# Another order of the side jobs in a long convolution, and the second normalisation of an MLP block one step sooner

## The chip, the cores and the metric

The kernel runs on one core of a Trainium2 chip. The metric is the device time of one execution in microseconds (us), the median of several runs. The engines are TensorE (PE in the profile, its weight loads PEld), VectorE (DVE), ScalarE (ACT), GpSimd (POOL) and SyncE (SP), which here only issues transfers.

## The reference

One transformer-like block on a sequence of S = 2048 rows and D = 640 channels, in float32. `mod` gives six rows of 640 from a condition vector.

```python
mod = (_silu(c) @ w_mod).reshape(c.shape[0], 6, 1, -1)
sa, ca, ga, sb, cb, gb = (mod[:, 0], mod[:, 1], mod[:, 2], mod[:, 3], mod[:, 4], mod[:, 5])
h = _layernorm(x, axis=-1) * (1 + ca) + sa
x = x + ga * _A_ref(h, A_k, A_v, A_shift_k, A_ssm_k, A_ssm_D)
h = _layernorm(x, axis=-1) * (1 + cb) + sb
x = x + gb * _B_ref(h, B_w1, B_b1, B_w2, B_b2)
```

`_A_ref` is a convolution: K goes through a causal convolution with four taps, is multiplied with V, and the product (kv) goes through a causal convolution as long as the sequence, one filter per channel, by FFT of length 4096; kv times a row D is added, and the result is multiplied with the normalised input. `_B_ref` is an MLP with 1728 hidden units: a matmul with w1, plus b1, ReLU, squared, a matmul with w2, plus b2.

## The kernel before

**Two stages.** The convolution stage treats the channels in five blocks of 128 (b = 0 to 4). The FFT is written as small matmuls with constant matrices. The MLP stage treats the rows in eight blocks of 256 (n = 0 to 7), and in each the hidden units in 14 steps (f = 0 to 13).

**The convolution of one block.** `unit_a` (line 383, `A` below) is one of eight transform units of a block: the filter's four (i = 1) and the data's four (i = 0), 64 small matmuls each into two PSUM tiles `pa`, which ACT copies to SBUF. `front` (eight per block) makes the spectra of filter (`h`) and data (`x`, line 398), ACT copies `h`, DVE multiplies twice, POOL subtracts and adds. `back` (four per block, line 464) is the first inverse transform and needs the products of two fronts. `unit_t` transposes (line 530, copied by ACT) and `unit_y` is the last inverse transform (line 541). In block 0 the filter's spectra are made ahead by `early_h`. The transform units of block b + 1 run in the tail of block b. In short, `A2.0.0` is the first data unit of block 2.

**Side jobs.** Everything else is a side job, called with its block and part. `kv_k`, `kv_v` transpose K and V on PE; `kv_s` applies the taps on DVE, `kv_m` multiplies and stores kv to DRAM; `kv_v` also issues the next loads of K and V. `load_h` and `load_x` load filter and kv of a block, for its transform units; `skip` adds the row D to the filter. `q_big`, `q_ut` load rows of q for `stats1`, the first normalisation's statistics; `stats1_end` takes the square root (line 303) and the reciprocal. `part_load`, `part_scale`, `part_add`, `mod_row`, `mod_col` compute the rows of `mod`. `load_xp`, `prep_a` (line 499, four ACTIVATEs), `prep_m`, `prep_p`, `gate`, `finish_near`, `finish_add` normalise q, gate the convolution's result and add it to q. `load_item`, `w_high`, `w_low` load the MLP's weights and split them into a high and a low part.

**What sets the order.** A table written out by hand gives the place of each side job: `FS(b, j)` is step j of the fronts of block b (j = 0 to 9), `GS(b, s)` is step s of its tail (s = 0 to 17). `UNITS` gives, per block, the tail steps of the transform units (seven; the eighth goes with step 9 of the fronts), of the eight `unit_t` and of the eight `unit_y`. In a tail step, `unit_y` and `unit_t` come first, then the transform units, then the table's jobs; for steps in `AFTER` the jobs come ahead of the transform units (in a step of the fronts, behind the `back`). At the end `keep_order` ties every engine's instructions to the order in which the program gave them. So each engine, and SP's queue with it, goes through its list in order, and an instruction that waits holds up those behind it.

**Queues and buffers.** All large transfers go through SP. `sp_dma` makes each transfer wait until the fourth one before it has landed:

```python
queued.append(nc.cur_bb.bb.instructions[-1].name)
if len(queued) > OUT:
    info = mybir.DependencyInfo(mybir.DependencyClass.Sync, mybir.DependencyReason.DATA)
    tc.add_manual_dep(nc.cur_bb.bb.instructions[-1], queued[-1 - OUT], info, reason="place in time")
```

PSUM has four buffers with the tag X (`pa`, `h`, `x`, V transposes), two with Y (`back`, `unit_y`, some K transposes) and two with T. The parts of `mod` and the staged weights share four SBUF buffers (tag STG). kv goes through two buffers, the halves of which `kv_k` writes and the store of `kv_m` frees.

**The MLP.** Step i of its loop issues the second matmuls of step i - 3 (`mlp_back`, line 790), the split of step i - 1's hidden values (`mlp_split`, an ACT copy into `hring` and a DVE subtraction), the first matmuls of step i (line 720, 15 of them), and their ReLU on ACT (line 752) and square on POOL. Beside them the next block is prepared: `load_x1` at f = 3, `stats2` at f = 5, square root and reciprocal at f = 6, then two `prep_hat` (line 672), each the normalisation of 128 rows, and from f = 8 on one `prep_xt` per step: two transposes on PE (line 685, one from each normalised half), scale and shift on DVE, split on ACT and POOL. In block 0 the two `prep_hat` are at f = 5 and 6, in the blocks n = 1 to 6 at f = 7 and 8.

## Time and profile before

| | |
|---|---|
| median of 3 runs | 703.28 us (702.06 to 704.84) |
| the profiled execution | 705.5 us, its span 703.7 us |
| convolution, MLP | up to about 292 us, from there to the end |
| TensorE busy | 662.0 us, 94% of the span |
| DVE, ACT, POOL busy | 334.6, 329.6, 311.2 us |
| granted TensorE clock, mean | 0.992 |
| moved by DMA | 74.76 MB |

The span runs from the first to the last instruction of the profiled execution; its time contains the little that lies around it. A row of the timeline gives the start, the duration, the engine and line, the operation with what it writes and reads, and how often it was merged; the brackets give how long the engine was idle before it and what ended the wait. "issue" stands for an idle engine that waits for nothing the profile shows.

### The profile page before, as it was taken

How to read it: one execution, taken by the hardware profiler on the slowest of the kernel's cores; microseconds unless marked ns; L12 is line 12 of the kernel's file. 1: busy time of each engine (PE TensorE's matmuls, PEld its weight loads, DVE VectorE, ACT ScalarE, POOL GpSimd, SP SyncE). 2: the span in 40 equal slices, each digit the busy share in tenths (PEclk: the TensorE clock that was granted, in tenths of full speed). 3: DMA queues.
4: the chain of work that ended last, by engine and by line, in shares of the span. 5: the costliest groups of instructions: out<-in, count | busy, mean ns of one | idle time of the engine just before them, and what ended most of it. 6: DMA issues, size and time to landing. Idle time of an engine off the chain costs nothing.

```text
span 703.7 us, 21084 instructions
## 1 busy us (share of the span) xinstructions
PE 662.0 (94%) x9164; PEld 634.2 (90%) x9164; DVE 334.6 (48%) x601; ACT 329.6 (47%) x688; POOL 311.2 (44%) x390
## 2 busy tenths in 40 slices
...
DMA packets 110960, 74.76 MB, mean 106 GB/s; under 512 B 48658, under 2 KB 96146, under 8 KB 110868
## 3 DMA queue, kind: packets, MB, share of 16 engines
...
## 4 chain that ended last, share of the span: by engine, by line
PE 83%; ACT 6%; DVE 5%; issue 3%; DMA 2%; POOL 1%; SPq 0%; DVEq 0%; ACTq 0%; POOLq 0%
PE acc L790 27%; PE h L720 25%; PE pa L383 5%; PE x L398 5%; PE qp L464 5%; PE y L541 5%; PE h L398 3%; PE t L530 2%; PE h L711 1%; PE xtp L685 1%; PE kt L239 1%; DVE wx L151 1%; ACT a L146 1%; PE vt L276 1%; PE gr L928 1%
## 5 line engine op out<-in xcount | busy, mean ns | idle before, releaser
L151 POOL TENSOR_TENSOR mtmp<-mtmp 128x256 f32<-128x256 f32 x112 | 71.4, 638 | 244.4 <-ACT mtmp L752 236.5
L720 PE MATMUL h<-xt,w_S 128*128 128x256 f32 x1290 | 167.5, 281 | 1.1 <-DVE w_S L157 1.1
L720 PEld LDWEIGHTS h<-xt,w_S 128*128 128x128 f32 x1290 | 161.7, 190 | 1.3 <-DVE w_S L157 1.3
L790 PE MATMUL acc<-w_S,hring 128*128 128x320 f32 x960 | 156.6, 311 | 0.2 <-DVE hring L157 0.2
L157 DVE TENSOR_TENSOR hring<-mtmp,hring 128x256 fp32r<-128x256 f32 x112 | 66.4, 593 | 162.6 <-ACT hring L146 162.6
L790 PEld LDWEIGHTS acc<-w_S,hring 128*128 128x128 f32 x960 | 142.0, 188 | 0.7 <-DVE hring L157 0.7
L752 ACT ACTIVATE mtmp<-h,b1t 128x256 f32<-128x256 f32 x104 | 49.4, 475 | 180.1 <-PE h L720 177.0
L146 ACT ACTIVATE hring<-mtmp 128x256 fp32r<-128x256 f32 x112 | 46.6, 416 | 48.5 <-POOL mtmp L151 47.5
L383 PE MATMUL pa<-wx,p 64*64 64x64 f32 x2560 | 49.7, 228 | 10.9 <-issue 5.3
L383 PEld LDWEIGHTS pa<-wx,p 64*64 64x64 f32 x2560 | 44.1, 141 | 17.2 <-issue 11.3
L146 ACT ACTIVATE a<-pa 128x512 f32<-128x512 f32 x80 | 43.6, 611 | 22.9 <-PE pa L383 22.8
L151 DVE TENSOR_TENSOR wx<-x,wx 128x512 f32<-128x512 f32 x64 | 41.0, 684 | 19.4 <-PE x L398 8.9
L541 PE MATMUL y<-wx,wx 128*64 128x64 f32 x1280 | 45.4, 226 | 4.5 <-ACT wx L146 2.7
L541 PEld LDWEIGHTS y<-wx,wx 128*64 128x64 f32 x1280 | 40.7, 139 | 9.5 <-issue 4.2
L687 DVE TENSOR_SCALAR we<-xtp,cbs 128x256 f32<-128x256 f32 x35 | 19.0, 544 | 61.1 <-PE xtp L685 61.1
L398 PE MATMUL x<-a,gb 128*64 128x128 f32 x640 | 43.8, 281 | 3.0 <-DVE wx L151 1.8
L398 PEld LDWEIGHTS x<-a,gb 128*64 128x64 f32 x640 | 37.7, 141 | 4.4 <-PE h L398 2.4
L261 DVE SCALAR_TENSOR_TENSOR KV<-kt,tap,KV 128x511 f32<-128x511 f32 (+2 forms) x48 | 35.9, 747 | 8.1 <-ACT ktail L146 6.3
L154 POOL TENSOR_TENSOR wm<-wm,wm 128x640 f32<-128x640 f32 x20 | 32.9, 1647 | 10.3 <-ACT wm L341 10.0
L146 ACT ACTIVATE q<-qp 128x512 f32<-128x512 f32 (+1 forms) x40 | 21.3, 585 | 33.1 <-PE qp L464 33.1
L157 POOL TENSOR_TENSOR we<-wx 128x256 f32<-128x256 f32 x20 | 15.8, 789 | 47.0 <-DVE wx L151 46.1
L398 PE MATMUL h<-a,gb 128*64 128x128 f32 x512 | 34.4, 275 | 0.6 <-ACT wx L146 0.6
...
## 6 DMA issues: line engine op xcount, KB each, us to landing
...
KV<-in_A_k_dram SPq DMA_DIRECT2D x20, 256.0 KB, 4.6
KV<-in_A_v_dram SPq DMA_DIRECT2D x20, 256.0 KB, 4.5
p<-in_A_ssm_k_dram SPq DMA_DIRECT2D x20, 256.0 KB, 4.9
p<-kv_d SPq DMA_DIRECT2D x20, 256.0 KB, 4.8
xp<-in_A_q_dram SPq DMA_DIRECT2D x20, 256.0 KB, 4.5
...
```

The source lines that it names most:

```text
L146: act.activation(o, i, AF.Copy)
L151: eng.tensor_mul(o, a, b)
L154: eng.tensor_add(o, a, b)
L157: eng.tensor_sub(o, a, b)
L261: dve.scalar_tensor_tensor(o, tk[:, : 512 - t], tap[:, b, t : t + 1], o, op0=ALU.mult, op1=ALU.add)
L383: pe.matmul(t[e][64 * r : 64 * r + 64, g].rearrange("p m d -> p (m d)"), pt[b][l, i, 8 * q + g, :], cw[l, r], start=True, stop=True,)
L398: pe.matmul(t[64 * a : 64 * a + 64, s + r], gb[:, g, r, a], AX[b][i][:, 2 * g + a], start=True, stop=True,)
L464: pe.matmul(t[a][:, u], gi[l, 4 * j + u, r], w[r][l, u % 2], start=(r == 0), stop=(r == 1),)
L541: pe.matmul(y[64 * h : 64 * h + 64, 4 * (g % 2) + i].rearrange("p c l d -> p (c l d)"), tss[g][:, i, 64 * r : 64 * r + 64], ca[:, r, h], s ...
L720: pe.matmul(hps[n, f][:m], WI[1, f][:, a, b], XT[n][:, x, b], start=(b == 0 and i == 0), stop=(b == NB - 1 and i == 2),)
L752: act.activation(r[:m], h[:m], AF.Relu, bias=b1t[:m, f : f + 1])
L790: pe.matmul(acc[2 * s + i], h[:, a, s * P : (s + 1) * P], w[:, y, i * 320 : (i + 1) * 320], start=(f == 0 and ti == 0), stop=(f == NF - 1 ...
```

## The change

In blocks n = 1 to 6 of the MLP both `prep_hat` calls stand in step f = 7. In the convolution about 110 of the side jobs stand in other steps or in another order within a step, seven more steps are in `AFTER` (20 become 27, not all the same), and `UNITS` has other steps for some transform units, `unit_t` and `unit_y`. No job is added or left out. The parts of the diff that the prediction speaks of:

```diff
@@ -938,140 +938,149 @@
...
-    at(FS(0, 1), (kv_k, 1, 0, "T"), (kv_v, 1, 0), (p_tile, 2))
-    at(FS(0, 2), (early_h, 0, 6))
-    at(FS(0, 3), (kv_s, 1, 0))
-    at(FS(0, 4), (early_h, 0, 7))
-    at(FS(0, 5), (kv_m, 1, 0), (kv_k, 1, 1, "T"))
-    at(FS(0, 6), (skip, 1))
-    at(FS(0, 7), (kv_s, 1, 1))
-    at(FS(0, 8), (kv_v, 1, 1))
-    at(FS(0, 9), (q_big, "XP0", 0))
-    at(GS(0, 0), (kv_m, 1, 1), (kv_k, 1, 2, "Y"), (kv_v, 1, 2), (q_big, "XP1", 4))
-    at(GS(0, 1), (kv_s, 1, 2))
-    at(GS(0, 2), (stats1, 0))
+    at(FS(0, 1), (early_h, 0, 6), (kv_k, 1, 0, "T"), (kv_v, 1, 0))
+    at(FS(0, 2), (p_tile, 2))
+    at(FS(0, 3), (early_h, 0, 7), (kv_s, 1, 0), (kv_m, 1, 0))
+    at(FS(0, 5), (skip, 1), (kv_k, 1, 1, "T"), (q_big, "XP0", 0))
+    at(FS(0, 8), (kv_s, 1, 1))
+    at(GS(0, 0), (kv_v, 1, 1), (kv_m, 1, 1), (kv_k, 1, 2, "Y"), (kv_v, 1, 2))
+    at(GS(0, 1), (kv_s, 1, 2), (stats1, 0))
+    at(GS(0, 2), (q_big, "XP1", 4))
...
-    at(FS(1, 1), (kv_k, 2, 2, "T"), (q_big, "UP1", 12), (stats1, 7))
-    at(FS(1, 2), (part_scale, 2, 0))
-    at(FS(1, 3), (skip, 2), (kv_s, 2, 2), (kv_v, 2, 2), (kv_m, 2, 2), (kv_k, 2, 3, "T"), (part_add, 2, 1, pool))
-    at(FS(1, 4), (kv_s, 2, 3), (kv_v, 2, 3), (part_scale, 2, 2), (part_load, 2, 4))
-    at(FS(1, 5), (kv_m, 2, 3), (part_add, 2, 2, pool), (part_scale, 2, 3), (part_load, 1, 0))
-    at(FS(1, 6), (q_ut,))
-    at(FS(1, 7), (part_add, 2, 3, pool))
-    at(FS(1, 8), (load_xp, 0))
-    at(FS(1, 9), (load_x, 2), (stats1, 13), (part_scale, 2, 4))
-    at(GS(1, 0), (p_tile, 3), (kv_k, 3, 0, "Y"))
-    at(GS(1, 1), (kv_s, 3, 0), (part_load, 1, 1))
+    at(FS(1, 2), (q_big, "UP1", 12), (part_scale, 2, 0), (part_load, 2, 4))
+    at(FS(1, 3),
+        (skip, 2), (kv_s, 2, 2), (kv_v, 2, 2), (kv_m, 2, 2), (kv_k, 2, 3, "T"), (q_ut,), (stats1, 7),
+        (part_add, 2, 1, pool),
+    )
+    at(FS(1, 5), (kv_s, 2, 3), (kv_v, 2, 3), (kv_m, 2, 3), (load_xp, 0), (part_scale, 2, 3))
+    at(FS(1, 6), (part_scale, 2, 2))
+    at(FS(1, 8), (stats1, 13), (part_add, 2, 2, pool), (part_load, 1, 0))
+    at(FS(1, 9), (part_scale, 2, 4))
+    at(GS(1, 0), (kv_k, 3, 0, "Y"), (part_add, 2, 3, pool), (part_add, 2, 4, pool))
+    at(GS(1, 1), (load_x, 2), (kv_s, 3, 0), (part_load, 1, 1))
...
     at(GS(1, 15),
-        (kv_m, 3, 3), (stats1, 8), (stats1, 10), (mod_row, 1), (part_scale, 0, 0), (part_scale, 0, 1),
-        (part_scale, 0, 2), (part_load, 0, 3), (part_load, 0, 4),
+        (kv_v, 3, 3), (kv_m, 3, 3), (mod_row, 1), (part_scale, 0, 0), (part_scale, 0, 1), (part_scale, 0, 2),
     )
-    at(GS(1, 16), (load_x, 3), (stats1_end,), (part_add, 0, 1, pool), (part_add, 0, 2, pool))
-    at(FS(2, 0), (load_h, 3), (load_xp, 1))
-    at(FS(2, 2), (part_scale, 0, 3), (prep_a, 0, 1))
-    at(FS(2, 3), (part_add, 0, 3, pool), (part_scale, 0, 4))
-    at(FS(2, 4), (part_add, 0, 4, pool), (prep_a, 0, 0), (prep_a, 0, 3), (prep_m, 0, 1))
-    at(FS(2, 5), (prep_m, 0, 0))
-    at(FS(2, 6), (skip, 3), (part_load, 3, 0), (part_load, 3, 2), (prep_a, 0, 2), (prep_m, 0, 3))
+    at(GS(1, 16), (stats1, 8), (part_add, 0, 2, pool), (part_load, 0, 4))
+    at(GS(1, 17), (load_h, 3), (stats1, 10), (load_xp, 1))
+    at(FS(2, 0), (load_x, 3), (part_scale, 0, 3))
+    at(FS(2, 1), (stats1_end,), (part_add, 0, 1, pool), (part_add, 0, 3, pool), (prep_a, 0, 1))
+    at(FS(2, 2), (part_scale, 0, 4))
+    at(FS(2, 3), (part_add, 0, 4, pool))
+    at(FS(2, 4),
+        (part_load, 3, 1), (prep_a, 0, 0), (prep_a, 0, 2), (prep_a, 0, 3), (prep_m, 0, 0), (prep_m, 0, 1),
+    )
+    at(FS(2, 5), (part_load, 3, 0), (prep_m, 0, 3))
...
-    at(GS(2, 1), (kv_s, 4, 0), (part_scale, 3, 1), (gate, 0, 1))
+    at(GS(2, 1), (p_tile, 4), (kv_s, 4, 0), (part_scale, 3, 1), (part_load, 3, 3), (gate, 0, 1), (gate, 0, 3))
...
-    at(GS(2, 14), (kv_v, 4, 3), (prep_a, 1, 3))
-    at(GS(2, 15), (prep_m, 1, 3), (gate, 1, 0))
-    at(GS(2, 16), (mod_col, 3, cbs[:, 0], 0.0), (part_load, 4, 1), (prep_p, 1, 3), (gate, 1, 1))
-    at(GS(2, 17), (kv_m, 4, 3), (part_load, 4, 3))
+    at(GS(2, 14), (kv_m, 4, 3))
+    at(GS(2, 15),
+        (mod_col, 3, cbs[:, 0], 0.0), (prep_m, 1, 2), (prep_a, 1, 3), (prep_m, 1, 3), (prep_p, 1, 3),
+        (gate, 1, 0),
+    )
+    at(GS(2, 16), (part_load, 4, 3), (prep_p, 1, 2), (gate, 1, 1))
+    at(GS(2, 17), (part_load, 4, 1))
...
-    AFTER = {GS(0, 9), GS(0, 11), GS(0, 14), GS(1, 1), GS(1, 4), GS(1, 12), GS(1, 13), GS(1, 14), FS(2, 9), GS(2, 1), GS(2, 2), GS(2, 9), GS(2, 10), GS(2, 15), GS(2, 17), GS(3, 2), GS(3, 5), GS(3, 10), GS(3, 12), GS(3, 16)}
+    AFTER = {GS(0, 3), GS(0, 4), GS(0, 6), GS(0, 9), GS(0, 11), GS(0, 14), GS(0, 15), GS(1, 1), GS(1, 3), GS(1, 7), GS(1, 8), GS(1, 10), GS(1, 11), GS(1, 13), GS(1, 14), GS(1, 15), FS(2, 9), GS(2, 4), GS(2, 9), GS(2, 15), GS(2, 17), GS(3, 1), GS(3, 2), GS(3, 4), GS(3, 12), GS(3, 14), GS(3, 15)}
     UNITS = [
-        ([0, 2, 4, 11, 11, 16, 16], [1, 3, 3, 5, 5, 6, 7, 9], [3, 4, 4, 6, 6, 8, 9, 10]),
-        ([1, 1, 5, 7, 9, 10, 12], [1, 3, 4, 6, 8, 11, 14, 14], [4, 6, 7, 10, 13, 14, 16, 17]),
-        ([1, 3, 5, 7, 8, 11, 14], [1, 3, 5, 7, 9, 11, 12, 15], [4, 6, 8, 9, 12, 14, 16, 17]),
-        ([0, 3, 4, 6, 9, 11, 14], [1, 3, 4, 7, 9, 11, 13, 14], [4, 6, 8, 10, 13, 14, 16, 17]),
-        ([], [1, 1, 2, 2, 5, 5, 6, 7], [4, 4, 5, 6, 6, 8, 8, 10]),
+        ([0, 1, 4, 11, 13, 16, 16], [1, 3, 3, 5, 5, 6, 7, 9], [3, 4, 4, 6, 7, 8, 8, 11]),
+        ([2, 2, 5, 5, 10, 10, 12], [1, 4, 4, 7, 8, 11, 13, 14], [4, 7, 7, 11, 13, 13, 16, 17]),
+        ([1, 2, 5, 7, 8, 11, 14], [1, 2, 5, 7, 9, 11, 13, 15], [4, 7, 8, 9, 13, 14, 16, 17]),
+        ([0, 3, 4, 6, 9, 11, 14], [1, 2, 4, 7, 8, 11, 14, 14], [4, 6, 8, 10, 11, 14, 17, 17]),
+        ([], [1, 1, 2, 2, 5, 5, 6, 6], [4, 5, 5, 6, 6, 8, 9, 9]),
     ]
...
@@ -1233,8 +1242,11 @@
                 if n and f == 6:
                     stats2_root(n + 1)
                     stats2_end(n + 1)
-                if f - (5 if n == 0 else 7) in (0, 1):
-                    prep_hat(n + 1, f - (5 if n == 0 else 7))
+                if n == 0 and f in (5, 6):
+                    prep_hat(1, f - 5)
+                if n and f == 7:
+                    prep_hat(n + 1, 0)
+                    prep_hat(n + 1, 1)
                 if f >= 8 and f - 8 < NB:
                     (prep_xt if n else prep_xt2)(n + 1, f - 8)
             if f >= 11 and f < 13:
```

164 lines of the change are left out of this document (86 added, 78 removed).

## The prediction

> **What bounds the kernel now.** I read the page's busy shares and the chain of waits first, then stretches of time, then who TensorE waits for.
>
> ```profile
> PE 662.0 (94%) x9164; PEld 634.2 (90%) x9164; DVE 334.6 (48%) x601; ACT 329.6 (47%) x688; POOL 311.2 (44%) x390
> PE 83%; ACT 6%; DVE 5%; issue 3%; DMA 2%; POOL 1%; SPq 0%; DVEq 0%; ACTq 0%; POOLq 0%
> 90.00:150.00 60.00, 57.19 (x1314) 51.25 (x1310) 39.57 (x78) 41.49 (x75) 32.44 (x45) 1.00 0.85 241
> 150.00:205.00 55.00, 52.72 (x1256) 47.87 (x1252) 39.34 (x61) 44.51 (x95) 45.25 (x52) 1.00 0.76 194
> 205.00:265.00 60.00, 56.73 (x1374) 52.27 (x1372) 46.36 (x59) 43.99 (x93) 48.66 (x47) 1.00 0.53 137
> 395.00:460.00 65.00, 63.68 (x488) 63.45 (x487) 20.82 (x43) 20.36 (x46) 21.70 (x27) 1.00 0.12 41
> ```
>
> (Columns of a stretch: its length, then busy time of PE, PEld, DVE, ACT, POOL, the granted clock, DMA share, GB/s.) TensorE is the bound everywhere. In the MLP (from 292 us on) the other engines are idle two thirds of the time, and 1.3 of 65 us are left on TensorE. In the convolution ACT, DVE and POOL are busy 54 to 82% as well, so an order can matter there; TensorE idles 2.3 to 3.3 us in each of these stretches. Only its idle time can be won, and the waits name it:
>
> ```profile
> PE xtp L685 <- ACT mtmp L672: 7.9, 6, 1.3
> PE pa L383 <- issue: 5.3, 5, 2.3
> PE y L541 <- ACT wx L146: 2.7, 4, 1.3
> PE x L398 <- DVE wx L151: 1.8, 3, 1.0
> ```
>
> (us in total, times, longest.) The largest, six times 1.3 us, is the place that the change's last hunk edits.
>
> **The MLP edit.** It removes nothing and adds nothing: the second of two `prep_hat` ACTIVATEs (line 672) is issued in step 7 of a block instead of step 8. The timeline of block 1, from step 7 to step 10, and the same wait one block later:
>
> ```profile
> 367.02 0.91 ACT L672 ACTIVATE mtmp<-x,nm,rs 128x640 f32<-128x640 f32 x1
> 367.85 0.42 ACT L146 ACTIVATE hring<-mtmp 128x256 fp32r<-128x256 f32 x1
> 368.15 1.93 PE L720 MATMUL h<-xt,w_S 128*128 128x256 f32 x15
> 370.18 0.47 ACT L752 ACTIVATE mtmp<-h,b1t 128x256 f32<-128x256 f32 x1 [1.91 <-PE h L720]
> 370.55 0.91 ACT L672 ACTIVATE mtmp<-x,nm,rs 128x640 f32<-128x640 f32 x1
> 371.51 0.33 PE L685 MATMUL xtp<-ident,mtmp 128*128 128x128 f32 x1 [1.32 <-ACT mtmp L672]
> 373.45 1.96 PE L720 MATMUL h<-xt,w_S 128*128 128x256 f32 x15
> 377.22 1.96 PE L720 MATMUL h<-xt,w_S 128*128 128x256 f32 x15
> 422.60 0.33 PE L685 MATMUL xtp<-ident,mtmp 128*128 128x128 f32 x1 [1.32 <-ACT mtmp L672]
> ```
>
> The second normalisation starts at 370.55 because it stands behind the ReLU of step 8, which waits for that step's matmuls; the transpose that reads it waits until 371.51. Step 8 lasts 373.45 - 368.15 = 5.30 us. Step 9 has the same 15 + 2 + 12 matmuls and lasts 377.22 - 373.45 = 3.77. The wait therefore costs 5.30 - 3.77 = 1.53 us per block, a little more than its 1.32 of shown idle. It occurs for n = 1 to 6, the six times of the wait row: block 0 keeps its old steps and the last block prepares nothing. Term: 6 x 1.53 = **-9.2 us**; the lower bound is the shown idle, 7.9.
>
> What hides the moved 0.91 us: after it ACT still has the split copy of step 7 (367.85 becomes 368.8) and then the ReLU at 370.18, before which it was idle 1.91 us. It now idles 1.0. The split copy is read by matmuls three steps later, some 10 us away, so nobody waits for it. With the cover gone, the ReLU itself would be late by the 0.91 and the wait would stay. The second normalisation is then ready at 368.8, and its transposes are wanted at 370.2: late next is nothing within 1.3 us.
>
> **The table of side jobs.** Laid side by side, the two orders have the same instructions on every engine; nothing is added or removed, DMAs included. On TensorE fewer than 20 of 211 groups change place. So the sum of work is unchanged and I cost places, from first to last.
>
> *End of the first front.* The value transposes of (1,1) stood ahead of the transform unit at 55.9 and now stand two units behind it; `early_h` and `kv_m(1,0)` come earlier on PE and DVE.
>
> ```profile
> 54.94 0.66 PE L276 MATMUL vt<-ident,KV 128*128 128x128 f32 x4
> 55.90 1.26 PE L383 MATMUL pa<-wx,p 64*64 64x64 f32 x64 [0.30 <-POOL p L154]
> 57.08 2.06 PE L464 MATMUL qp<-wx,gi 64*128 64x128 f32 x32
> 56.48 0.72 POOL L154 TENSOR_TENSOR wx<-wx 128x256 f32<-128x256 f32 x1
> ```
>
> The inverse matmuls at 57.08 need POOL's last product, done at 57.20 for their second half; it cannot be ready much earlier. Without the transposes TensorE arrives earlier, waits for POOL all the same, and pays their 0.5 afterwards: +0.5; up to +0.9 if `kv_m(1,0)`, now ahead of front 4 on DVE, passes its delay to POOL. `skip(1)` one step sooner takes the 0.30 away, but into the same wait.
>
> *The stall at 75 to 77 us.* It hangs on a store, through ACT:
>
> ```profile
> 63.77 3.07 SPq L138 DMA_DIRECT2D q<-in_A_q_dram  x4
> 68.53 0.33 SPq L138 DMA_DIRECT2D kv_d<-KV  x1
> 73.22 0.69 ACT L241 ACTIVATE KV<-kt,tap 128x512 f32<-128x512 f32 x1 [2.69 <-DMA kv_d<-KV]
> 75.00 1.15 PE L541 MATMUL y<-wx,wx 128*64 128x64 f32 x32 [1.29 <-ACT wx L146]
> 77.00 1.64 PE L541 MATMUL y<-wx,wx 128*64 128x64 f32 x32 [0.85 <-ACT wx L146]
> KV<-in_A_v_dram SPq DMA_DIRECT2D x20, 256.0 KB, 4.5
> ```
>
> ACT's order there is unchanged, and so is SP's last part: four q loads, then the store of (1,2), which by the rule of four in flight waits for the first of them. What changes is what that first q load waits for: the value load that goes out after the displaced transposes. They end near 57.1 + 2.0 + 1.1 + 0.6 = 60.8 instead of 55.6, and a value load lands 4.5 us later (the last row, a median). That puts the q load at 65.3 at the latest and the store 0 to 1.5 us later. The delay above ends in this same stall, so the two overlap: together **+0.9** (0 to +1.5).
>
> *The square root.* `stats1_end` moves from ahead of the third block's first front to behind its second.
>
> ```profile
> 146.72 1.28 ACT L303 ACT_TABLE_LOAD   x1
> 148.02 0.31 ACT L303 ACTIVATE rs<-st,eps_t 128x16 f32<-128x16 f32 x1
> 149.36 1.09 PE L398 MATMUL h<-a,gb 128*64 128x128 f32 x16 [0.55 <-ACT wx L146]
> 150.78 1.09 PE L398 MATMUL x<-a,gb 128*64 128x128 f32 x16 [0.32 <-DVE wx L151]
> 157.80 3.18 ACT L499 ACTIVATE KV<-xp,nm,rs 128x128 f32<-128x128 f32 x8
> 168.07 2.06 PE L464 MATMUL qp<-wx,gi 64*128 64x128 f32 x32
> ```
>
> Before, 148.33 - 146.72 = 1.6 us of ACT delay the first two copies of the block, and TensorE waits 0.55 + 0.32 = 0.87; at the MLP's ratio of lost to shown time (1.53 to 1.32) that is 1.0. Moved, the 1.6 delays the copy of the third front, whose four PSUM buffers come round again only two fronts later; TensorE needs some 3.5 us for two fronts and doesn't wait. But in step 4 twelve ACTIVATEs of `prep_a` now stand together where eight took 3.18: 4.8 us, so the copy of front 5 comes 1.6 later, and DVE, POOL and the inverse matmuls up to 168.07 follow it. Part of that meets slack; I take half of the 1.0 as kept: **-0.5** (-1.0 to +1.6, the last if the 1.6 is paid whole and the 1.0 not won). The Trainium skill, ScalarE: Activation LUTs, What ACT_TABLE_LOAD costs, counts a drain of some 1.4 us with each table load. The trace differs: the square root follows its load after 1.30. By the page I estimate the third copy 1.4 us later still and the term at about +0.5; the sum would be -8.6.
>
> *Small ones.* At two places the operation that ACT did ahead of the awaited one now comes behind it: `part_scale(3,1)` and the last `prep_a(1,3)`.
>
> ```profile
> 175.44 0.66 PE L276 MATMUL vt<-ident,KV 128*128 128x128 f32 x4 [0.43 <-ACT a L146]
> 198.81 1.15 PE L541 MATMUL y<-wx,wx 128*64 128x64 f32 x32 [0.36 <-ACT wx L146]
> ```
>
> **-0.8** (0 to -0.8).
>
> *Units due sooner.* `A2.0.0` follows `A2.1.3` directly, while `load_x(2)` goes from front step 9 to tail step 1 and `part_load(2,4)` waits for a buffer that POOL frees.
>
> ```profile
> 117.08 4.88 SPq L138 DMA_DIRECT2D p<-kv_d  x4
> 122.82 1.16 PE L383 MATMUL pa<-wx,p 64*64 64x64 f32 x64
> p<-kv_d SPq DMA_DIRECT2D x20, 256.0 KB, 4.8
> ```
>
> The transfers ahead of `load_x(2)` in SP's order are the same set, so it goes out near 117 as before; its first quarter lands near 117.1 + 4.8 = 121.9 and is wanted at 123.9. Zero, with 2 us in hand. The other moves (gates, loads, `finish_add`) I followed on each queue and found covered: DVE, ACT and POOL each have nearly 10 us or more free in every stretch quoted. "issue" stalls (5.3 us at `pa`) fall on dense runs of small matmuls; pairs are split here and joined there: 0, +-1.5.
>
> Sum for the convolution: 0.9 - 0.5 - 0.8 = -0.4; with the MLP -9.2 - 0.4 = **-9.6 us**: the profiled span goes from 703.7 to 694.1, its execution from 705.5 to 695.9. That execution lies 0.3% above the median of 703.28, within what runs scatter (702.06 to 704.84); the difference applied to the median gives **693.7 us**.
>
> **Rivals.** (1) *The new order removes most of the convolution's waits.* Those of the rows above (2.7 and 1.8 in the list, 0.55, 0.43 and 0.30 singly) sum to 5.8 us; with all gone, 703.3 - 9.2 - 5.8 = 688.3. For it: they are short and made by order. Against: 2.1 of them, at 75 to 77 us, hang on an unchanged order. 0.15. (2) *Side jobs in front of awaited copies on ACT eat most of the gain.* Each such place costs about the 1.6 us of the twelve ACTIVATEs; with four to five uncovered ones, 6 to 8 us, it is 700 to 702. For it: ACT is busy 44.5 of 55 us at 150 to 205. Against: ACT's order shifts by one or two places only. 0.08. (3) *SP is held.* If `part_load(2,4)` or `part_load(1,0)` waits for POOL longer than I read, key loads, `load_xp(0)` and `load_x(2)` all shift, and TensorE pays each us beyond the 2 in hand at `A2.0.0`. It decides the sign from a hold of 9.6 + 2 = 11.6 us; with 16, the time is 703.3 - 9.6 + 14 = 707.7. For it: both wait on adds that stand behind fronts on POOL. Against: those adds need no later load, and POOL idles 27 of 60 us from 90 to 150. 0.05. (4) *The edit doesn't remove the wait*, because the input of the second normalisation is late too: 703. Against: the first reads the same tile and statistics at 367.02 with no wait shown. 0.02.
>
> **Numbers.** The forecast has 0.70. Its own range is 690 to 699: the bounds above, from -1.8 to +3.1 together, and 1.5 of issue stalls either way. For 8 in 10 I reach over much of (1) and stop short of (2): 688.5 to 699. About 0.5% (3.5 us) is what a measurement here can tell from no change. Faster by more: 0.70 + 0.15 + a fifth of (2) = 0.87; same: 0.08; slower: 0.05.
>
> **What would show it.** Right: the wait of `xtp` for line 672 vanishes from TensorE's waits; step 8 lasts 3.8 us; line 672 runs twice in a row before the split copy; DVE's wait for `xtp` shrinks in no other step. The waits at 149 to 151 go, those at 75 to 77 stay, the store of (1,2) goes out at 68.5 to 70. Wrong: MLP blocks still last 422.60 - 371.51 = 51.1 us; or the convolution's end moves by more than 4 us either way; or `pa` waits for the kv_d loads near 124.

## The result, and the profile after

The changed kernel takes 692.89 us (median of 4 runs, 692.28 to 696.13); the kernel before, run beside it, 704.06 us (702.06 to 705.56). The ratio is 0.9857, with a 95% interval of 0.9826 to 0.9889: faster by 1.4%, with 1 outside the interval, and 0.8 us below the forecast. The profiled execution took 693.38 us, its span 691.6.

From the page of the changed kernel its busy times and the chain of waits; then its stretches of time, columns as in the prediction; then TensorE's waits:

```profile
PE 657.0 (95%) x9164; PEld 630.8 (91%) x9164; DVE 335.9 (49%) x601; ACT 330.1 (48%) x688; POOL 311.4 (45%) x390
PE 81%; DVE 6%; ACT 5%; DMA 4%; issue 2%; POOL 1%; DVEq 0%; POOLq 0%; ACTq 0%; SPq 0%
```

```profile
90.00:150.00 60.00, 53.93 (x1266) 48.51 (x1264) 38.40 (x75) 37.30 (x68) 30.75 (x43) 1.00 0.83 232
150.00:205.00 55.00, 53.76 (x1274) 48.55 (x1272) 44.17 (x63) 45.36 (x97) 46.94 (x51) 1.00 0.86 226
395.00:460.00 65.00, 65.00 (x498) 65.00 (x497) 20.82 (x45) 20.94 (x47) 20.77 (x28) 1.00 0.11 41
```

```profile
PE pa L383 <- issue: 6.1, 6, 2.0
...
PE pa L383 <- DMA p<-kv_d: 3.1, 2, 2.3
...
PE h L398 <- ACT wx L146: 1.5, 1, 1.5
```

Before, the list of waits was led by `xtp` with 7.9 us; now it has no row for `xtp` at all, and TensorE is busy for all 65 us of an MLP stretch instead of 63.68. In the convolution the wait of `h` for ACT's copy has grown from 0.6 to 1.5 us and moved on by one front, and from 90 to 150 us TensorE is busy 3.3 us less than before (the same stretch of time holds partly other work). On the chain ACT gives up a per cent and DMA takes two more. The timeline of block 1 of the MLP, answering to the one shown of before:

```profile
363.81 0.47 ACT L752 ACTIVATE mtmp<-h,b1t 128x256 f32<-128x256 f32 x1 [1.97 <-PE h L720]
364.18 1.73 ACT L672 ACTIVATE mtmp<-x,nm,rs 128x640 f32<-128x640 f32 x2
365.31 1.93 PE L720 MATMUL h<-xt,w_S 128*128 128x256 f32 x15
367.08 0.38 PE L685 MATMUL xtp<-ident,mtmp 128*128 128x128 f32 x2
367.34 0.48 ACT L752 ACTIVATE mtmp<-h,b1t 128x256 f32<-128x256 f32 x1 [1.12 <-PE h L720]
369.06 1.96 PE L720 MATMUL h<-xt,w_S 128*128 128x256 f32 x15
```

Both normalisations run in one row of 1.73 us and are ready at 365.91, 1.17 us before the first transposes at 367.08. Step 8 lasts 369.06 - 365.31 = 3.75 us; it was 5.30. From one block's first `xtp` to the next one's it is now 49.54 us, before 51.09.

Where the MLP begins, first before, then after (name, count, shortest, median and longest in ns, first and last start). I take the start of the `gr` matmuls, which make the MLP's gate row, as the border; the 292 us of the prediction are where they end:

```profile
L928 PE MATMUL gr<-w_gate x20: 432/432/537, 285.0 to 291.4; 128*128 128x320 f32 x20
```

```profile
L928 PE MATMUL gr<-w_gate x20: 432/432/537, 282.2 to 288.5; 128*128 128x320 f32 x20
```

From there to the end of the span it is 703.7 - 285.0 = 418.7 us before and 691.6 - 282.2 = 409.4 after: **-9.3 us in the MLP, -2.8 us in the convolution** by this pair of profiles. The second number isn't what it seems. The granted clock differs between these two executions in the early convolution (the number after the five busy times), first before, then after:

```profile
36.00:62.00 26.00, 25.32 (x468) 23.12 (x472) 15.88 (x25) 10.08 (x22) 14.38 (x27) 0.93 0.79 227
62.00:90.00 28.00, 23.47 (x692) 21.47 (x684) 19.11 (x41) 15.65 (x30) 3.88 (x12) 0.94 0.86 247
```

```profile
36.00:62.00 26.00, 25.50 (x542) 23.56 (x543) 17.97 (x29) 11.85 (x24) 15.63 (x31) 1.00 0.85 237
62.00:90.00 28.00, 24.58 (x680) 22.38 (x680) 18.60 (x41) 17.45 (x33) 4.70 (x14) 1.00 0.92 252
```

One pair of profiles cannot tell the order's part from the clock's part. The first experiments take the two halves of the change apart and give more executions of each order.

### The profile page after: what moved, and what is told of

The parts are those of the page before. It is cut to its first block, busy times and chain, and to the rows that moved or that the text cites. A ratio compares the mean times of both kernels' runs of the same rounds, so it can differ in the third digit from the quotient of the medians.

```text
span 691.6 us, 21100 instructions
## 1 busy us (share of the span) xinstructions
PE 657.0 (95%) x9164; PEld 630.8 (91%) x9164; DVE 335.9 (49%) x601; ACT 330.1 (48%) x688; POOL 311.4 (45%) x390
## 3 DMA queue, kind: packets, MB, share of 16 engines
q8 instruction: 72, 1.18, 0.7%
## 4 chain that ended last, share of the span: by engine, by line
PE 81%; DVE 6%; ACT 5%; DMA 4%; issue 2%; POOL 1%; DVEq 0%; POOLq 0%; ACTq 0%; SPq 0%
PE acc L790 27%; PE h L720 26%; PE qp L464 5%; PE pa L383 4%; PE x L398 4%; PE y L541 4%; PE h L398 3%; DMA wm<-in_w_mod_dram 3%; PE t L530 2%; PE h L711 1%; PE xtp L685 1%; DVE KV L261 1%; ACT wx L146 1%; DVE kacc L261 1%; PE vt L276 1%
## 5 line engine op out<-in xcount | busy, mean ns | idle before, releaser
L541 PE MATMUL y<-wx,wx 128*64 128x64 f32 x1280 | 43.9, 224 | 2.9 <-ACT wx L146 1.6
L398 PE MATMUL x<-a,gb 128*64 128x128 f32 x640 | 41.6, 274 | 3.3 <-DVE wx L151 2.1
L398 PEld LDWEIGHTS x<-a,gb 128*64 128x64 f32 x640 | 35.9, 137 | 4.9 <-PE h L398 3.0
L790 PE MATMUL acc<-w_WX,hring 128*128 128x320 f32 x192 | 31.4, 312 | 0.0
```

Source lines behind the costliest of these rows:

```text
L398: pe.matmul(t[64 * a : 64 * a + 64, s + r], gb[:, g, r, a], AX[b][i][:, 2 * g + a], start=True, stop=True,)
L541: pe.matmul(y[64 * h : 64 * h + 64, 4 * (g % 2) + i].rearrange("p c l d -> p (c l d)"), tss[g][:, i, 64 * r : 64 * r + 64], ca[:, r, h], s ...
L790: pe.matmul(acc[2 * s + i], h[:, a, s * P : (s + 1) * P], w[:, y, i * 320 : (i + 1) * 320], start=(f == 0 and ti == 0), stop=(f == NF - 1 ...
```

## The experiments

**The MLP edit alone.** The kernel before with only the last hunk:

```diff
-                if f - (5 if n == 0 else 7) in (0, 1):
-                    prep_hat(n + 1, f - (5 if n == 0 else 7))
+                if n == 0 and f in (5, 6):
+                    prep_hat(1, f - 5)
+                if n and f == 7:
+                    prep_hat(n + 1, 0)
+                    prep_hat(n + 1, 1)
```

> The kernel before with the last hunk alone: both second-half and first-half normalisations of the MLP's blocks 1 to 6 in step 7, the table of side jobs as before. Theory A (the MLP edit does what the prediction says, independent of the convolution): -9.2 us, ratio 0.987 (0.9855 to 0.9885); the stretch from the first gr matmul to the end is 409.4 us instead of 418.7, and TensorE has no wait for xtp left. Rival B (the whole gain of the change is made in the MLP, and the convolution's 2.8 us in the two profiles are only the lower granted clock of the profile before): -11.2 us, ratio 0.984. Beside it this run is a second look at the unchanged convolution: by A the first gr matmul starts at 284 to 285 us whatever the clock, by B at 282 to 283 once the clock is full.

Measured: ratio 0.9889 (0.985 to 0.9928). The `gr` matmuls begin at 284.3 us and the span is 693.7, so the MLP takes 409.4 us, to 0.1 us what it takes in the changed kernel. Theory A holds; B's 0.984 is just outside the interval.

**The table alone.** The changed kernel with the old `prep_hat` lines put back (the same hunk reversed).

> The changed kernel with the old place of the second normalisation (step 8), so only the table of side jobs and the units are changed. The prediction's sum for this part: -0.4 us, ratio 0.9994. By the two traces (start of the MLP at 282.2 instead of 285.0): -2.8 us, ratio 0.996. Rival (those 2.8 us were the granted clock of 0.93 and 0.94 in the profile before, between 36 and 90 us): 0, ratio 1.000. The waits at TensorE for the load of wm ahead of the second front's copy (1.46 us at 149.6) are in its profile in any case.

Measured: ratio 0.9979 (0.9953 to 1.0005), on 704.14 us some -1.5 us (-3.3 to +0.4). The prediction's -0.4 and the -2.8 of the two profiles are both inside; 0 is as well. The profiled execution is the longest of 12 (708.03 us), and the same convolution that ended at 282.2 above ends later than before the change:

```profile
L928 PE MATMUL gr<-w_gate x20: 432/432/537, 287.5 to 293.9; 128*128 128x320 f32 x20
```

The MLP takes 706.3 - 287.5 = 418.8 us, as before the change. So the MLP repeats to 0.1 us, and the convolution alone scatters by over 5.

**Place or step?** The kernel before, with the second normalisation still in step 8 but ahead of that step's ReLU:

```diff
+            if 0 < n < NC - 1 and f == 8:
+                prep_hat(n + 1, 1)
             mlp_front_end(n, f)
...
-                if f - (5 if n == 0 else 7) in (0, 1):
-                    prep_hat(n + 1, f - (5 if n == 0 else 7))
+                if n == 0 and f in (5, 6):
+                    prep_hat(1, f - 5)
+                if n and f == 7:
+                    prep_hat(n + 1, 0)
```

> The kernel before with the second normalisation still in step 8, but issued ahead of that step's ReLU and not behind it. Theory A (the wait is made by the place behind the ReLU in ScalarE's order): the same -9.2 us as the step sooner, ratio 0.987, no xtp wait, because it starts at about 368.3 in block 1 and is ready at 369.2, a us before its transposes are wanted at 370.2. Rival (a whole step of lead is needed, because its input or its buffer isn't free before): the xtp wait stays at 0.5 to 1.3 us in each of six blocks, ratio 0.992 to 1.000.

Measured: ratio 0.9889 (0.985 to 0.9927), span 693.7 with `gr` from 284.3, so 409.4 us again. ScalarE's order in block 1:

```profile
367.15 0.42 ACT L146 ACTIVATE hring<-mtmp 128x256 fp32r<-128x256 f32 x1
367.48 0.91 ACT L672 ACTIVATE mtmp<-x,nm,rs 128x640 f32<-128x640 f32 x1
369.48 0.47 ACT L752 ACTIVATE mtmp<-h,b1t 128x256 f32<-128x256 f32 x1 [1.10 <-PE h L720]
```

The normalisation fills time in which ScalarE waited for the step's matmuls. Its place behind the ReLU made the wait, not the step it is written in.

**How much cover there is.** The changed kernel with the second normalisation of step 7 issued one to three times more:

```diff
                     prep_hat(n + 1, 0)
                     prep_hat(n + 1, 1)
+                    for _ in range((n + 1) // 2):
+                        prep_hat(n + 1, 1)
```

> The changed kernel with the second normalisation of step 7 issued again, with the same result, once more in blocks 1 and 2, twice more in blocks 3 and 4, three times more in blocks 5 and 6 (0.87 us of ScalarE each). It measures the cover that the moved 0.9 us was said to have. Theory A (free up to the 1.1 to 1.2 us that ScalarE is idle ahead of the next ReLU and that the transposes have in hand): blocks 1 and 2 as long as in the changed kernel, blocks 3 and 4 longer by 0.6 to 0.8, blocks 5 and 6 by 1.5 to 1.7, xtp waits of 0.6 and 1.4. Rival (the matmuls read the late split copy or the late square sooner than three steps on): blocks 1 and 2 longer already. Rival (the transposes alone set it, the ReLU's delay is seen by nobody): the same lengths as in theory A, and no wait of TensorE but that for xtp.

Measured, from the first `xtp` of one block to that of the next: 49.54 and 49.56 us in blocks 1 and 2 (one more), 50.27 and 50.28 in blocks 3 and 4 (two more), 51.25 in block 5 (three more): +0, +0.7 and +1.7. TensorE's waits from the MLP's begin on:

```profile
PE xtp L685 <- ACT mtmp L672: 4.0, 4, 1.5
PE h L720 <- DVE w_S L157: 1.1, 1, 1.1
PE acc L790 <- DVE hring L157: 0.2, 1, 0.2
```

The sizes are those of theory A; the last two rows are in the changed kernel's profile with the same numbers. The only wait that grows is that for `xtp`. In the trace the ReLU of step 8 begins 2.72 us after its matmuls in block 3 and 3.67 in block 5, against 2.03 in the changed kernel (367.34 - 365.31), so it is 0.7 and 1.6 us late, and TensorE has no wait for that. So the third reading in the expectation fits: the transposes set the limit. What a late ReLU would cost alone was not tested, since TensorE is held about as long by the transposes.

**The changed kernel once more.**

> The changed kernel once more, for its scatter and a second profile: 692 to 696 us, ratio 0.986; from the first gr matmul to the end 409.4 us as in its first profile (an MLP without waits repeats to 0.1 us), its convolution's end anywhere from 281 to 288 us. If the granted clock sets the scatter, the profile with the lower clock between 36 and 90 us has the later end; if the stalls without a shown cause set it, the one with more of them.

Measured: ratio 0.9853 (0.9801 to 0.9906); span 695.4, `gr` from 286.0, so 409.4 again. The table gives, from the timelines of seven profiles, the time between the starts of the same matmuls. The last two columns are the sum of TensorE's waits marked "issue" from 40 us to the end of the convolution (to 0.1 us), and the granted clock from 36 to 62 and from 62 to 90 us.

| profile | up to block 3's first K transposes | block 1's tail, to the first front of block 2 | head of block 2, to its last inverse matmuls | from there to `gr` | `gr` | issue | clock |
|---|---|---|---|---|---|---|---|
| old order: before | 116.59 | 28.51 | 22.97 | 116.96 | 285.03 | 6.4 | 0.93, 0.94 |
| old: the MLP edit alone | 115.68 | 28.10 | 22.71 | 117.85 | 284.34 | 5.4 | 0.93, 1.00 |
| old: ahead of the ReLU | 115.55 | 28.20 | 22.71 | 117.87 | 284.33 | 5.6 | 1.00, 0.94 |
| new order: after | 111.50 | 31.19 | 24.75 | 114.73 | 282.17 | 5.6 | 1.00, 1.00 |
| new: after, once more | 114.91 | 28.51 | 23.97 | 118.58 | 285.97 | 7.4 | 0.91, 1.00 |
| new: the table alone | 117.39 | 29.97 | 21.77 | 118.39 | 287.52 | 8.8 | 0.93, 0.99 |
| new: normalisation repeated | 116.83 | 26.97 | 23.97 | 116.00 | 283.77 | 6.2 | 1.00, 0.93 |

Among the four of the new order the clock of 36 to 62 us and the stalls go with the end alike, so both readings of the expectation stand; the two were not separated. Variants that follow below say that neither alone accounts for the end: two with the full clock there end at 285.9 us, with 7.6 and 7.7 us of stalls (the square root in the gap, the additions later), and one with 4.7 us of stalls ends at 286.7, with a clock of 0.93 (the data load sooner). The means of `gr` are 284.6 for the old order and 284.9 for the new one. No gain of the new table shows here: it gains a little in the first and the last stretch and loses 0.8 to 0.9 us each, on the mean, in block 1's tail and in the head of block 2. The next experiments look for why. Timelines of the changed kernel (its first profile) at the places that they touch:

```profile
54.49 2.19 PE L464 MATMUL qp<-wx,gi 64*128 64x128 f32 x32
54.89 0.72 POOL L154 TENSOR_TENSOR wx<-wx 128x256 f32<-128x256 f32 x1
66.10 0.74 SPq L138 DMA_DIRECT2D kv_d<-KV  x1
72.24 1.15 PE L541 MATMUL y<-wx,wx 128*64 128x64 f32 x32 [0.60 <-ACT wx L146]
120.43 1.17 PE L383 MATMUL pa<-wx,p 64*64 64x64 f32 x64 [0.82 <-DMA p<-kv_d]
131.57 1.61 ACT L341 ACTIVATE wm<-wm,sg 128x640 f32<-128x640 f32 x2 [2.80 <-DMA wm<-in_w_mod_dram]
148.19 0.83 ACT L341 ACTIVATE wm<-wm,sg 128x640 f32<-128x640 f32 x1 [2.98 <-DMA wm<-in_w_mod_dram]
149.52 1.28 ACT L303 ACT_TABLE_LOAD   x1
149.56 1.09 PE L398 MATMUL h<-a,gb 128*64 128x128 f32 x16 [1.46 <-ACT wx L146]
150.82 0.31 ACT L303 ACTIVATE rs<-st,eps_t 128x16 f32<-128x16 f32 x1
```

**A scaling ahead of an awaited copy.** At 148.19 ScalarE stood 2.98 us at the load of part (0,3), with the copy of block 2's second front behind it; TensorE lost 1.46 us.

```diff
-    at(FS(2, 0), (load_x, 3), (part_scale, 0, 3))
-    at(FS(2, 1), (stats1_end,), (part_add, 0, 1, pool), (part_add, 0, 3, pool), (prep_a, 0, 1))
+    at(FS(2, 0), (load_x, 3))
+    at(FS(2, 1), (part_scale, 0, 3), (stats1_end,), (part_add, 0, 1, pool), (part_add, 0, 3, pool), (prep_a, 0, 1))
```

> The changed kernel with one job moved: the scaling of part (0,3) of the modulation, whose load lands at 148.2, stands behind the copy of block 2's second front instead of ahead of it. Theory S (each us that ScalarE stands at that load ahead of an awaited copy is paid by TensorE, and what follows the copy has slack, as the prediction said of the square root): the waits of 1.46 and 0.32 at 149.6 and 151.0 vanish, -1.8 us against the changed kernel. Theory D (the slack behind is used up: the scaling, the table load, the square root and the first four normalisations then hold the copy of the third front, which ends at about 153.4 instead of 153.9): only -0.5 us, the fifth front starts at about 153.4 instead of 154.0 and waits for the copy.

Measured: ratio 0.9892 (0.9858 to 0.9925), no gain in time. The waits at 149.6 and 151.0 are gone and the part up to the first inverse matmuls lasts 7.09 us instead of 9.31. But the fifth front now waits, and the part behind it lasts 16.88 instead of 15.44:

```profile
156.81 1.09 PE L398 MATMUL h<-a,gb 128*64 128x128 f32 x16 [1.33 <-ACT wx L146]
```

Of 2.2 us won 1.4 are given back at once. The head of block 2 is 0.8 us shorter, near theory D's 0.5 and not S's 1.8. That the edit took the first two waits away is not shown: the three other profiles of the new order in the table have the same 7.09 us without it. In the second profile of the changed kernel the scaling starts at 145.01 without a wait, because its load has landed by then.

**Why the third front's copy is late.** In that profile and in the second one of the changed kernel the copy stands behind four normalisations of q that wait for DVE. From the second profile of the changed kernel:

```profile
148.74 0.72 POOL L157 TENSOR_TENSOR we<-wx 128x256 f32<-128x256 f32 x1
148.80 2.88 DVE L305 SCALAR_TENSOR_TENSOR nm<-st,rs 128x16 f32<-128x16 f32 x1
149.43 0.72 POOL L154 TENSOR_TENSOR we<-wx 128x256 f32<-128x256 f32 x1
150.12 3.14 POOL L154 TENSOR_TENSOR wm<-wm,wm 128x640 f32<-128x640 f32 x2
151.72 1.65 ACT L499 ACTIVATE KV<-xp,nm,rs 128x128 f32<-128x128 f32 x4 [3.23 <-DVE nm L305]
153.89 1.09 PE L398 MATMUL h<-a,gb 128*64 128x128 f32 x16 [1.33 <-ACT wx L146]
```

The DVE operation has 16 columns; it took 0.28 us in the first profile of the changed kernel (from 151.45), here 2.88. It ends at 151.68, and the first of POOL's two additions, which lasts 1.53 us by itself, at 150.12 + 1.53 = 151.65. The experiment is the previous one with these two additions behind the products of the third and fourth fronts:

```diff
-    at(FS(2, 1), (part_scale, 0, 3), (stats1_end,), (part_add, 0, 1, pool), (part_add, 0, 3, pool), (prep_a, 0, 1))
+    at(FS(2, 1), (part_scale, 0, 3), (stats1_end,), (prep_a, 0, 1))
...
-    at(FS(2, 3), (part_add, 0, 4, pool))
+    at(FS(2, 3), (part_add, 0, 1, pool), (part_add, 0, 3, pool), (part_add, 0, 4, pool))
```

> The kernel of e4 with two of POOL's additions (parts (0,1) and (0,3)) behind the products of block 2's third and fourth fronts instead of ahead of them. In the profiles of e4 and of the second run of the changed kernel the small DVE operation nm<-st,rs (0.28 us in one profile) takes 2.17 and 2.88 us and ends with POOL's first addition, to 0.01 us; ScalarE's normalisation waits for it, the copy of the third front stands behind that, and TensorE waits 1.33 us at the fifth front. Theory P (DVE is held while POOL runs without a gap): nm ends with POOL's last product of the second front instead, 1.5 us sooner, lasts under 1 us, and the wait at the fifth front falls from 1.33 to 0.2 or none. Rival Q (the operation waits for something else, the square root's result or its own queue): nm as long as before, wait 1.3.

```profile
150.85 0.72 POOL L154 TENSOR_TENSOR we<-wx 128x256 f32<-128x256 f32 x1
150.94 0.67 DVE L305 SCALAR_TENSOR_TENSOR nm<-st,rs 128x16 f32<-128x16 f32 x1
164.84 0.49 PE L464 MATMUL qp<-we,gi 64*128 64x128 f32 x4 [0.72 <-POOL we L157]
```

`nm` takes 0.67 us and ends at 151.61, 0.04 behind POOL's last product; the wait at the fifth front is gone. This is what theory P forecast, and Q is out, since `nm` ends with POOL and not with the root. P's wording, that DVE is held while POOL runs without a gap, is too strong, though. In the first profile of the changed kernel POOL goes on without a gap as well:

```profile
150.97 0.73 POOL L157 TENSOR_TENSOR we<-wx 128x256 f32<-128x256 f32 x1 [2.42 <-DVE wx L151]
151.65 0.73 POOL L154 TENSOR_TENSOR we<-wx 128x256 f32<-128x256 f32 x1
```

There `nm` ends at 151.73, behind the first of these two (151.70). In all 14 profiles it ends at most 0.05 us behind the end of a POOL instruction: in ten of them behind the first end after its start (0.28 to 0.67 us), in four behind the second or third (2.17 to 2.88). In those four the way from block 2's first inverse matmuls to its second lasts 7.35 or 7.36 us; in the three others with the change's order at this place (the first profile, the table alone, and the last experiment below) 5.6 to 5.9. What decides at which end it gets through is not shown, and since it also gets through early with the additions in their place, this one profile doesn't show that their move shortened it. The time is not won all the same: the additions now delay POOL's products of later fronts, TensorE waits 1.1 us for them around 165, and the head of block 2 lasts 24.2 us. Ratio 0.9893 (0.9849 to 0.9937), from two runs. The Trainium skill, SBUF — State Buffer, section SBUF: two separate sides, says that a DVE operation with two SBUF inputs and a GpSimd operation that reads SBUF take a shared port by an exclusive lock for a whole instruction. The trace agrees in kind. In the second profile of the changed kernel it shows more than one instruction's wait: 2.88 us, over three POOL instructions that follow each other without a gap.

**The square root in the gap.** The changed kernel with the square root behind the first front's copy and the normalisations later:

```diff
-    at(FS(2, 0), (load_x, 3), (part_scale, 0, 3))
-    at(FS(2, 1), (stats1_end,), (part_add, 0, 1, pool), (part_add, 0, 3, pool), (prep_a, 0, 1))
+    at(FS(2, 0), (load_x, 3), (stats1_end,))
+    at(FS(2, 1), (part_scale, 0, 3), (part_add, 0, 1, pool), (part_add, 0, 3, pool))
...
-    at(FS(2, 3), (part_add, 0, 4, pool))
+    at(FS(2, 3), (part_add, 0, 4, pool), (prep_a, 0, 1))
```

> The changed kernel with the head of block 2 rearranged on ScalarE: the square root stands behind the copy of the first front, where ScalarE waits for the load of part (0,3) anyway; the scaling of that part stands behind the second front's copy and the first four normalisations of q behind the fourth front's. Theory D (it is what stands ahead of the copies of the second and third fronts that TensorE pays for): no wait at the fourth and fifth fronts, the stretch from block 2's first front to its first inverse matmuls 7.1 to 7.6 us (9.3 in the changed kernel's trace) and on to the third inverse matmuls no more than 14.7, so -2 us against the changed kernel. Rival G (the gain is given back at the next wait, as 1.35 of 2.35 us was with the scaling moved alone): -0.5 us or less.

Measured: the part to the first inverse matmuls lasts 7.09 us without a wait, so here the square root costs TensorE nothing. But the rest of the head lasts 16.08, not 14.7: the twelve normalisations of step 4 (4.73 us in a row) hold the copy of the sixth front until TensorE waits 0.75. Ratio 0.9857 (0.9813 to 0.9901), as the changed kernel: rival G.

**The middle undone.** The changed kernel with the old jobs, `AFTER` entries and units from `FS(1, 1)` to `FS(2, 9)`:

```diff
-    at(FS(1, 2), (q_big, "UP1", 12), (part_scale, 2, 0), (part_load, 2, 4))
...
+    at(FS(1, 1), (q_big, "UP1", 12), (stats1, 7))
+    at(FS(1, 2), (part_scale, 2, 0))
...
-        ([2, 2, 5, 5, 10, 10, 12], [1, 4, 4, 7, 8, 11, 13, 14], [4, 7, 7, 11, 13, 13, 16, 17]),
+        ([1, 1, 5, 7, 9, 10, 12], [1, 3, 4, 6, 8, 11, 14, 14], [4, 6, 7, 10, 13, 14, 16, 17]),
```

> The changed kernel with the middle of the table undone: from front step 1 of block 1 to front step 9 of block 2 all side jobs and the transform units of block 1's tail stand as in the kernel before; the rest of the table and the MLP as changed. Theory M (the new order loses time here: three traces of it need 31.2, 30.0 and 31.8 us from the first K transposes of block 3 to the first front of block 2, three of the old order 28.5, 28.1 and 28.2, and the head of block 2 another 0.7 more): -2.7 to -3.4 us against the changed kernel, the first stretch back at 28 to 28.5. Rival N (the difference is what single executions scatter, and TensorE's stretches are set by transfers that take their time in either order): 0, ratio to the kernel before as that of the changed one, 0.986.

Measured: block 1's tail 27.40 us, the head of block 2 22.51, `gr` from 281.7. In the profile theory M has it right, at the two places named. In the times nothing is left of it: ratio 0.9873 (0.9824 to 0.9922).

**Old middle, new head.** The same with the square root behind the first front's copy of block 2 and the other two jobs later:

```diff
-    at(GS(1, 16), (load_x, 3), (stats1_end,), (part_add, 0, 1, pool), (part_add, 0, 2, pool))
-    at(FS(2, 0), (load_h, 3), (load_xp, 1))
-    at(FS(2, 2), (part_scale, 0, 3), (prep_a, 0, 1))
-    at(FS(2, 3), (part_add, 0, 3, pool), (part_scale, 0, 4))
+    at(GS(1, 16), (load_x, 3), (part_add, 0, 1, pool), (part_add, 0, 2, pool))
+    at(FS(2, 0), (load_h, 3), (load_xp, 1), (stats1_end,))
+    at(FS(2, 2), (part_scale, 0, 3))
+    at(FS(2, 3), (part_add, 0, 3, pool), (part_scale, 0, 4), (prep_a, 0, 1))
```

> The kernel of e5 (middle of the table undone) with the square root behind the first front's copy of block 2, the scaling of part (0,3) behind the third front's, and the first four normalisations of q behind the fourth front's. By the terms seen so far: block 1's tail 27.4 to 28.5 us as in e5 and the old order, block 2's head 7.1 us to the first inverse matmuls (8.0 in e5) and 14.5 to 14.7 on to the fourth, so -1 us against e5 and -2 to -3 against the mean of the changed kernel's profiles: ratio to the kernel before 0.982. Rival: the terms are real in the profile and lost in the scatter of whole executions, or given back on the way to 206 us: ratio 0.985 to 0.987 as e5 and the changed kernel.

Measured: tail 28.01, head 7.08 + 15.27 = 22.35, `gr` from 281.6; ratio 0.988 (0.9837 to 0.9923). The head won 0.2 us against the kernel above, not 1, and the rival has the time right. The two `gr` of 281.7 and 281.6 are the earliest of all 14 profiles, but both profiled executions lie below the median of their kernel's runs (692.87 against 696.67 us, 692.83 against 694.58). No version here is shown to be faster than the changed kernel.

**What holds block 1's tail.** Two more edits of the changed kernel. First, the data load of block 2 sooner in SP's order:

```diff
-    at(FS(1, 5), (kv_s, 2, 3), (kv_v, 2, 3), (kv_m, 2, 3), (load_xp, 0), (part_scale, 2, 3))
+    at(FS(1, 5), (kv_s, 2, 3), (kv_v, 2, 3), (kv_m, 2, 3), (part_scale, 2, 3))
...
-    at(FS(1, 8), (stats1, 13), (part_add, 2, 2, pool), (part_load, 1, 0))
+    at(FS(1, 8), (stats1, 13), (part_add, 2, 2, pool), (load_x, 2), (part_load, 1, 0))
...
-    at(GS(1, 1), (load_x, 2), (kv_s, 3, 0), (part_load, 1, 1))
+    at(GS(1, 1), (kv_s, 3, 0), (part_load, 1, 1))
...
-    at(GS(1, 3), (p_tile, 3))
+    at(GS(1, 3), (p_tile, 3), (load_xp, 0))
```

> The changed kernel with block 2's data load (load_x(2), for the unit A2.0.0) ahead of part_load(1,0) and of the first load_xp in SP's order; load_xp(0) comes behind it. In five profiles of the changed order the first of its transfers goes out at 115.3 to 117.9 us, whenever TensorE arrives, and TensorE waits 0.8 to 1.3 us for it where it arrives early. Theory L (the place in SP's queue is what makes it late): it goes out at 109 to 112, TensorE has no wait for p<-kv_d there, and block 1's tail lasts 0.8 to 2 us less where TensorE arrives before 114. Rival R (the stretch is paced by the w_mod loads that ScalarE's scalings wait for, which this puts later): the tail as long as before or longer, with longer waits of ScalarE for wm.

```profile
110.83 1.41 SPq L138 DMA_DIRECT2D kv_d<-KV  x1
114.78 3.36 SPq L138 DMA_DIRECT2D p<-kv_d  x4
133.48 1.62 ACT L341 ACTIVATE wm<-wm,sg 128x640 f32<-128x640 f32 x2 [3.78 <-DMA wm<-in_w_mod_dram]
135.64 0.66 PE L276 MATMUL vt<-ident,KV 128*128 128x128 f32 x4 [2.42 <-ACT a L146]
```

Theory L fails: with SP's queue free of other loads the data load still goes out at 114.78. Directly ahead of it stands the store of the kv that it reads back, and SP waits 2.5 us there for that store to land. The tail lasts 31.08 us, ScalarE stands 3.78 us at a `wm` load, and TensorE 2.42 at ScalarE. That is nearer to rival R; but ScalarE's waits for `wm` sum to 4.0 us between 112 and 142, no more than the 4.2 of the changed kernel's first profile. Ratio 0.9898 (0.9869 to 0.9928). Second, two of the scalings behind the units:

```diff
-    at(GS(1, 8), (kv_k, 3, 2, "Y"), (part_scale, 1, 2))
-    at(GS(1, 9), (stats1, 9), (part_scale, 1, 4), (part_load, 0, 0))
-    at(GS(1, 10), (kv_s, 3, 2), (part_add, 1, 2, pool), (part_add, 1, 4, pool))
+    at(GS(1, 8), (kv_k, 3, 2, "Y"))
+    at(GS(1, 9), (stats1, 9), (part_load, 0, 0))
+    at(GS(1, 10), (part_scale, 1, 2), (part_scale, 1, 4), (kv_s, 3, 2), (part_add, 1, 2, pool), (part_add, 1, 4, pool))
```

(`GS(1, 10)` is also taken out of `AFTER`.)

> The changed kernel with two scalings of modulation parts, (1,2) and (1,4), behind the two transform units of step 10 of block 1's tail instead of two steps sooner and ahead of them on ScalarE. In the profiles of the new order ScalarE waits 0 to 4.7 us in block 1's tail (112 to 142 us) for loads of wm that stand ahead of copies, in the old order at most 0.4; the tail lasts 27.0 to 31.8 against 27.4 to 28.5. Theory R (these waits, ahead of copies that TensorE needs, are what the new order loses there): no wait of ScalarE over 1 us ahead of the a copies, TensorE waits for ScalarE's a or up copies less than 0.5 us, the tail 27 to 29 us, ratio to the kernel before 0.982 to 0.985. Rival V (the loads come late whatever stands where; the wait moves to a scaling further on and the stalls without a shown cause stay): the tail 29 to 31.5 us, ratio 0.986 to 0.990.

```profile
130.25 1.55 ACT L341 ACTIVATE wm<-wm,sg 128x640 f32<-128x640 f32 x2 [2.09 <-DMA wm<-in_w_mod_dram]
132.35 0.66 PE L239 MATMUL kt<-ident,KV 128*128 128x128 f32 x4 [1.21 <-ACT up L146]
```

The two moved scalings wait for nothing any more, but the two before them (parts (1,1) and (1,0)) do, for 2.09 us, and TensorE 1.21 behind them. The tail lasts 30.33 us and the ratio is 0.9869 (0.9832 to 0.9907). These are the numbers of rival V, but not its mechanism: the wait is at scalings that stand sooner, which the edit left alone, and not further on. So theory R is not excluded. That the new order has ScalarE stand at `wm` loads in this tail is shown: 2.1 to 4.7 us between 112 and 142 us in seven profiles of it and its variants, 0 and 0.8 in the two others, at most 0.9 in the five with the old order there. The length of the tail goes with them: 30.0 to 31.8 us in the seven, 28.5 and 27.0 in the two, 27.4 to 28.5 in the five. That these waits can be taken away by one edit, or that they alone make the tail longer, is not shown.

## Why the prediction was right, and where it was not

**The MLP edit** was right in its mechanism and in its size. Predicted -9.2 us as 6 x 1.53; measured -9.3, as 409.4 against 418.7 us in every profile of either kind, 1.55 per block. ScalarE idles 1.12 us ahead of the ReLU where 1.0 was predicted, and the normalisation is ready 1.17 us ahead where 1.3 was. One sentence gave the wrong reason: that without cover "the ReLU itself would be late by the 0.91 and the wait would stay". With 0.87 us more it costs nothing; with 1.73 more the wait does come back, at the transposes, which wait for their input, and no wait for the late ReLU shows.

**The convolution's sum** of -0.4 us stands: the table alone measured -1.5 (-3.3 to +0.4), and the seven profiles have their ends at 284.6 and 284.9 us on the mean. Its terms do not, so that the sum came out is luck: the misses below are -1.4, +1.3, +0.8 and the 0.9 us of a tail that was not in it, and the first and last stretch of the table gain 0.8 and 0.6 us on the mean. The distance of 0.8 us from the forecast is luck as well, since six later runs of the changed kernel lie between 690.62 and 699.89 us.

- *End of the first front and stall at 75 to 77 us, predicted +0.9.* For the old order only the profile with the normalisation ahead of the ReLU has the full clock from 36 to 62 us; beside it stands the changed kernel's first. From the first `x` matmuls at 36 us to the first `y` it is 24.68 us in the old and 24.19 in the new: -0.5, not the +0.5 to +0.9 of the prediction. From the second inverse matmuls on (48.48 us before, 46.95 after) to the same `y` it is 14.2, 14.6 and 14.2 us in the three profiles of the old order and 13.7 to 13.8 in the four of the new one, so this gain repeats. The step that failed is "TensorE arrives earlier, waits for POOL all the same". In the rows above, POOL's last product ends at 55.61, 1.12 us after the inverse matmuls began at 54.49, and they took 2.19 us instead of 2.06. Evidently only the last of them need it. The stall was kept as predicted, 0.4 to 1.6 us and 0.85 in the new profiles, 1.1 to 1.3 and 0.85 in the old. The store went out 5.4 us after the first `y` (66.10 - 60.69) against 5.8 before: not later, though at 66.1 and not at 68.5 to 70.
- *The square root, predicted -0.5 (-1.0 to +1.6).* The head of block 2 takes 22.8 us on the mean in the old order and 23.6 in the new: +0.8, with 21.8 to 24.8 in single profiles. The gain at the first fronts came: up to the first inverse matmuls the old order takes 8.2 to 8.5 us, the new one 7.09 in three of four profiles. The twelve normalisations cost less than the bound of 1.6: from the second inverse matmuls to the third it is 5.63 us in the old order and 5.8 to 6.3 in the new. The step that failed is that what moves behind the second front "delays the copy of the third front" by 1.6 us, which TensorE doesn't see. I counted the table load and the root. I left out that the scaling of part (0,3) now stands ahead of the second front's copy with a load that lands at 148.2, and that four normalisations behind the root wait for `nm`, which POOL can hold back. "The waits at 149 to 151 go" was right where the load is in time (the second profile) and wrong where it isn't (the first). The root followed its table load by 1.30 us again (149.52 to 150.82). The larger cost by the Trainium skill (ScalarE: Activation LUTs, What ACT_TABLE_LOAD costs) would have given +0.5 by the prediction's estimate, nearer in size but with a cause that these rows do not show.
- *Small ones, predicted -0.8.* Both waits are gone from the new order's profiles (and from one of the old order's three), but others of the same size came: in the first one 0.30 us at a `y` for DVE near 182 and 0.64 at inverse matmuls for POOL near 212. About 0.
- *Units due sooner, predicted 0 with 2 us in hand.* The data load goes out at 114.8 to 119.0 us in eight profiles of the new order and its variants, near the 117 predicted. TensorE waits 0.82 us for it in the first profile, where it arrives 3 to 6 us sooner than in the other three of the table, and not at all in those. The prediction took TensorE's arrival as fixed.
- *What was missed:* ScalarE's waits for `wm` loads in block 1's tail. I checked each queue for its order and its free time, and found "nearly 10 us or more free" on ACT. Free time does not help an engine that goes in order and stands at a late load.
- *Stalls without a shown cause, predicted 0 +-1.5:* 5.4 to 6.4 us in the old order's three profiles, 5.6 to 8.8 in the new order's four. Their spread of 3.2 us stands beside one of 5.4 in the four ends.

**The rivals.** (1), most waits gone, did not come: the named waits stay and change places. (2) is what happened in kind, uncovered side jobs ahead of awaited copies, but at 1 to 3 us and balanced by gains elsewhere. (3)'s place showed a wait, of 0.8 us and not 14. (4) is excluded by the absent `xtp` row. The "wrong" sign named in the prediction, `pa` waiting for its load near 124, did appear (120.43) and cost that little.

**What stays open:** whether the table gains anything. An effect of 1 to 3 us lies inside the interval of every run here. The changed kernel has the ratios 0.9857 and 0.9853, the two kernels with the old table and the MLP's wait removed 0.9889 both; the intervals overlap. What paces block 1's tail, apart from ScalarE's waits and the stalls, was not separated.
